# Banded attention into a maxout layer, on one core: the hand-written unit queue is replaced by another order of the same units, with other engines named for 100 of them

## The chip, the core and the metric

The kernel runs on one core of one Trainium2 chip. The time is device microseconds of that core. TensorE (PE) multiplies and transposes, with its weight loads (PEld) beside it; VectorE (DVE), ScalarE (ACT) and GpSimd (POOL) copy, cast and do arithmetic; SyncE (SP) issues nearly all DMAs. Each engine takes its instructions strictly in program order, and semaphores hold it where its input or its buffer is not ready.

## The reference

The inputs are q, k and v in float32, with 4 batches, 8 heads, 768 positions and 64 values per head. A position attends to itself and the 95 before it, and to the 8 first positions. A bias falls linearly with distance, with a slope for each head. The attention result, 3072 tokens by 512, goes through a layer that takes the largest of three products, and through one more product.

```python
scores = scale * (q @ k.T) - slope[h] * dist          # kept where global or local
a = softmax(scores)                                   # over 768 keys, most are masked
x = (a @ v).transpose(0, 2, 1, 3).reshape(3072, 512)
h = maximum(maximum(x @ w1, x @ w2), x @ w3)          # 512 -> 768
out = h @ w_out                                       # 768 -> 512
```

## The kernel before, in words

The 3072 tokens are 24 **tiles** of 128, six to a batch. Tiles 0, 6, 12 and 18 open a batch and need only their own keys; the others need the tile before as well, whose first 8 keys are overwritten with the 8 global ones. For the last layer tiles are put together in seven **chunks** of 4, 2, 2, 4, 4, 4 and 4 tiles (chunks 0 to 6 start at tiles 0, 4, 6, 8, 12, 16 and 20).

The whole program is one list of small **units** in `SCHEDULE`, read from left to right (L475 to L476). Each unit is a letter, its indices, and for many a last digit that names an engine or a way. The order of the list is the order in which each engine gets its instructions. Nothing reorders them later. The letters:

- `l`, `L`, `v`, `w`, `o` (L151 to L174, L412 to L422): loads on SP. `l` n.s is a quarter or half of the q and k of a group of tiles (0 and 1; 2 and 3; 4 and 5; 6 to 9; 10 and 11); `L` is q and k of one tile from 12 on, as two DMAs of 256 KB; `v` is the v of a tile, 256 KB; `w` and `o` are the weights. The loads `l0.0` and `l0.1` stand ahead of the list.
- `c`, `C`, `W`, `Q`: casts to bf16 by the engine of the last digit (0 ACT, 1 DVE, 2 POOL; with C of q and k, 3 is one half by DVE and one by POOL). `C`T.0 casts q and k of tile T, `C`T.1 its v.
- `x` (L226) and `X` (L245): q and k turned so that the head dimension lies on partitions. `x`, and `X` with a last digit below 4, is 8 PE transposes into PSUM and copies out of it (`X` 3 and `x` 4 split the copy between ACT and DVE). `X`T.4 is one DMA transpose issued by SP (L250).
- `S` T.g (L268): scores of tile T for 4 heads (g 0 or 1) and their exponential on ACT (L288). With a last digit 1 PE first adds the bias by two more matmuls (L275); with 0 DVE multiplies by a mask of exponentials afterwards, in `M` T.g (L302).
- `A` T (L311): 8 or 16 small matmuls P times v; DVE then takes a reciprocal and scales into `xb` (L331, L332). The last digit is the PSUM region, shared with `S` of that g, so `S` T.g waits for the DVE of an `A` there, and the reverse.
- `T` T (L335): the tile of `xb` turned into a chunk's `xT`, by 4 PE transposes and a copy (0 ACT, 1 DVE), or with 4 by a DMA transpose from SP (L340).
- `F` c.f.j (L355): 4 matmuls of chunk c for 128 columns f of weight matrix j. j = 0 is copied out by ACT (L366); j = 1 and 2 are maxima on DVE (L368, L370). A PSUM buffer, of three, is free again only then.
- `O` c.t (L385): 6 matmuls of a tile with w_out, a copy by the named engine (L382), a store by SP. `E` is the last chunk's four tiles.
- `G`, `V` put the global keys and values in place (L216, L221); `K` and `B` (L291, L297) make masks and biases from a table of distances (L451 to L470); `D` lets PE multiply zeros three times at the start.

Buffers that the steps below touch: 3 PSUM buffers `psH` for F, O and half of the transposes; one for `psT`; one each for `sp0` and `sp1`; 6 for raw q and k, 6 for raw v, 3 for `xb`.

Of the kernel before, what the change touches and what calls it, by code (L numbers as in the profile page):

```python
# [22 lines left out]


SCHEDULE = """
    K0 K1 K2 K3 K4 K5 l1.0 l1.1 D0.3 c0.0.2 B0.1 B1.1 B2.1 B3.0 K6 B4.1 B5.1 c0.1.1 c1.0.2 x0.0.4 B6.1
    B7.1 x0.1.4 S0.0.1 v0 l2.0 l2.1 K7 S0.1.1 G0.0 S1.0.1 S1.1.0 x1.0.3 c1.1.2 M0.0 M0.1 M1.0 v1 x1.1.4
    C0.1.2 v2 A0.1 G1.2 S2.0.1 M1.1 c2.0.2 x2.0.1 C1.1.1 S2.1.0 G2.2 S3.0.1 M2.0 M2.1 C2.1.1 T0.1 S3.1.1
    M3.0 M3.1 c2.1.2 v3 A1.0 C3.1.0 w0.0 V1.2 x2.1.2 w1.0 A2.1 V2.2 A3.0 T1.0 T2.1 T3.1 W1.0.1 W0.0.0
    G3.2 S4.0.0 S4.1.0 F0.0.0 F0.1.0 M4.0 F0.2.0 F0.3.0 G4.1 S5.0.0 M4.1 S5.1.0 w0.1 W0.1.1 w0.2 W0.2.2  # L30
    V3.2 F0.0.1 F0.1.1 F0.0.2 F0.1.2 v4 C4.1.0 A4.0 V4.2 w1.1 W1.1.2 W2.0.0 F0.4.0 F0.5.0 M5.0 M5.1 w1.2
    W1.2.2 v5 W2.1.0 T4.0 F0.2.1 F0.3.1 l3.0 l3.2 F0.4.1 l3.1 c3.0.2 c3.2.2 F0.5.1 o2 C5.1.0 A5.1 l3.3
    F0.2.2 Q2.2 F0.3.2 W2.2.0 o0 T5.0 F0.4.2 o1 F0.5.2 x3.0.0 F1.0.0 F1.1.0 c3.1.1 F1.2.0 x3.2.0 Q0.2
    F1.0.1 F1.1.1 F1.2.1 l4.0 l4.1 c3.3.0 F1.0.2 F1.1.2 F1.2.2 x3.1.2 x3.3.1 F1.3.0 F1.4.0 Q1.2 F1.3.1
    S6.0.0 S6.1.0 v6 v7 v8 G6.0 F1.3.2 F1.5.0 v9 c4.0.1 F1.4.1 S7.0.0 S7.1.0 G7.2 v10 M6.0 M6.1 M7.0
    M7.1 O0.0.0 F1.4.2 c4.1.1 C6.1.2 C7.1.2 L12 F1.5.1 S8.0.0 S8.1.0 x4.0.0 O0.1.0 A6.0 x4.1.2 A7.1 V7.2
    F1.5.2 v11 T6.0 O0.2.0 T7.1 G8.2 C8.1.2 S9.0.0 S9.1.0 G9.1 v12 v13 O0.3.0 F2.0.0 F2.1.0 S10.0.0 M8.0
    M8.1 M9.0 M9.1 S10.1.0 C9.1.2 L13 L14 F2.0.1 F2.1.1 F2.0.2 A8.0 C12.0.1 F2.1.2 G10.2 O1.0.0 V8.2
    A9.1 X12.1 M10.0 M10.1 C10.1.0 C11.1.0 F2.2.0 S11.0.0 S11.1.0 M11.0 M11.1 L15 F2.3.0 F2.4.0 O1.1.0
    V9.2 A10.1 F2.2.1 V10.2 T8.0 F2.3.1 F2.5.0 T9.0 A11.1 F2.4.1 T10.0 F2.2.2 F2.3.2 T11.1 F2.4.2  # L40
    S12.0.0 S12.1.0 F2.5.1 C13.0.2 C14.0.2 C15.0.1 X13.4 F3.0.0 F3.1.0 F3.0.1 G12.1 C12.1.0 F3.2.0
    F3.1.1 F3.2.1 S13.0.0 S13.1.0 F2.5.2 v14 C13.1.0 C14.1.2 M12.0 M12.1 F3.0.2 F3.1.2 X14.4 F3.2.2
    X15.4 G13.2 M13.0 M13.1 S14.0.0 S14.1.0 F3.3.0 F3.4.0 F3.5.0 M14.0 M14.1 G14.1 A12.0 A13.1 F3.3.1
    F3.4.1 F3.5.1 S15.0.0 M15.0 S15.1.0 G15.0 v15 V13.2 L16 L17 v16 T12.4 v17 M15.1 O2.0.0 C15.1.0 A14.0
    V14.2 F3.3.2 F3.4.2 T13.4 F3.5.2 C16.1.0 C16.0.2 X16.3 T14.4 C17.0.2 A15.1 X17.4 O2.1.0 S16.0.0
    S16.1.0 G16.1 L18 V15.2 L19 T15.1 M16.0 O3.0.0 M16.1 F4.0.0 F4.1.0 F4.0.1 F4.1.1 C18.0.2 L20 C19.0.2
    A16.1 F4.2.0 F4.3.0 S17.0.0 S17.1.0 F4.2.1 F4.0.2 F4.3.1 v18 M17.0 v19 M17.1 X18.3 X19.4 C20.0.0
    V16.2 F4.1.2 C17.1.2 O3.1.1 A17.1 F4.2.2 F4.3.2 S18.0.0 M18.0 S18.1.0 M18.1 F4.4.0 T16.4 T17.4
    F4.4.1 C18.1.2 C19.1.1 F4.4.2 X20.4 G18.1 S19.0.0 S19.1.0 F4.5.0 L21 M19.0 M19.1 v20 F4.5.1 A18.0
    T18.4 F4.5.2 A19.1 T19.4 V19.1 C21.0.1 X21.4 G19.1 L22 C22.0.2 L23 X22.4 O3.2.1 O3.3.0 O4.0.1  # L50
    S20.0.0 S20.1.0 M20.0 G20.0 O4.1.0 F5.0.0 F5.1.0 F5.2.0 S21.0.0 S21.1.0 G21.2 F5.0.1 F5.1.1 M20.1
    M21.0 F5.3.0 F5.0.2 F5.1.2 F5.2.1 F5.2.2 v21 C20.1.1 C21.1.2 F5.4.0 S22.0.0 M21.1 S22.1.0 C23.0.0
    F5.3.1 M22.0 M22.1 F5.5.0 F5.3.2 A20.0 V20.2 G22.2 v22 F5.4.1 X23.4 v23 F5.5.1 T20.4 A21.1 V21.1
    T21.4 F5.4.2 F5.5.2 S23.0.0 S23.1.0 M23.0 O4.2.0 M23.1 C22.1.2 A22.0 C23.1.0 O4.3.0 V22.2 T22.4
    A23.1 T23.4 O5.0.1 O5.1.0 O5.2.1 O5.3.0 F6.0.0 F6.1.0 F6.0.1 F6.0.2 F6.2.0 F6.3.0 F6.4.0 F6.1.1
    F6.2.1 F6.1.2 F6.3.1 F6.4.1 F6.2.2 F6.3.2 F6.5.0 F6.4.2 F6.5.1 F6.5.2 E
"""


# [450 lines left out]
```

## Time and profile before

| what | value |
|---|---|
| median of 3 runs | 180.5 us (180.32 to 180.64) |
| span of the profiled execution | 178.5 us |
| what lies around the span (median less span) | 2.0 us |
| instructions | 3963 |
| ACT, DVE, POOL busy | 103.2, 119.1, 37.4 us |
| loads and stores | 35.52 MB, mean 199 GB/s |
| DMA transposes: xT, qkT | 11, 9 |

The time of the profiled execution itself is not given; its span is 178.5 us, and I set it beside the median. The page cuts the span into 40 slices of 4.46 us, with a digit for the busy tenths of each engine. "Idle before" in the groups is the time in which an engine had nothing to run just before an instruction of that group, with the engine or DMA that ended it. PE's busy time is of pipelined matmuls: a matmul is listed as 379 ns long while the next one starts 216 ns later, so I count PE by starts, not by durations.

### The profile page before, as it was taken

Reading aid. Unit: us, or ns where it says so; the run is one execution under the profiler, and the core shown is the slowest. Engines: PE = TensorE matmul, PEld = TensorE weight load, DVE = VectorE, ACT = ScalarE, POOL = GpSimd, SP = SyncE. Lnnn points to the kernel's source line nnn. Section 1 sums busy time; section 2 is a strip of 40 time slices with the busy share of each in tenths; the row PEclk is TensorE's granted clock in tenths of the full one; section 3 lists DMA queues with packets and bytes.
Section 4 is the critical chain, followed back from the end, with each engine's and each line's share of the span. In section 5 each row is a group of like instructions: output and inputs, shape, how many; then the busy total and the mean of one; then the engine's idle time right before and its main releaser. Section 6 shows DMA issues by size and latency. Waiting matters only on the chain.

```text
span 178.5 us, 3963 instructions
## 1 busy us (share of the span) xinstructions
PE 167.1 (94%) x1529; PEld 95.9 (54%) x1551; DVE 119.1 (67%) x237; ACT 103.2 (58%) x160; POOL 37.4 (21%) x65
## 2 busy tenths in 40 slices
PE   3599799999999999999999999999999999999991
PEld 0455645458866677845555555454454555444451
DVE  4519975977796689748978448978358986137610
ACT  4867898646689958555753936351862543440131
POOL 4255203543343012210006024100020401000000
PEclk9999999999999999999999999999999999999998
DMA  5999999999998899899544999988989664700015
GB/s 139 292 270 243 357 321 383 319 361 356 252 194 229 218 254 227 142 204 234 92 90 122 167 253 231 145 172 152 182 156 300 123 129 147 252 12 4 0 47 190
DMA packets 83587, 35.52 MB, mean 199 GB/s; under 512 B 66160, under 2 KB 78320, under 8 KB 83568
## 3 DMA queue, kind: packets, MB, share of 16 engines
q1 hardware_dynamic: 83424, 35.20, 83.6%
q8 instruction: 12, 0.20, 0.5%
q10 hardware_dynamic: 144, 0.07, 0.1%
q14 instruction: 7, 0.06, 0.1%
HBM read 25.17 MB, written 6.29 MB: 176 GB/s over the span
## 4 chain that ended last, share of the span: by engine, by line
PE 88%; ACT 3%; DVE 2%; POOL 2%; issue 1%; DMA 1%; POOLq 0%; ACTq 0%
PE h L361 53%; PE po L376 16%; PE sp L283 7%; PE op L322 3%; PE op L325 3%; PE tpp L239 3%; PE xtp L349 2%; ACT wmask L300 2%; PE sp L275 2%; DMA out_dram<-ost 1%; DVE qkT L243 1%; DVE xb L332 1%; ACT ost L382 1%; ACT P L288 1%; PE tp L261 1%
## 5 line engine op out<-in xcount | busy, mean ns | idle before, releaser
L361 PE MATMUL h<-xT,w 128*128 128x512 bf16 (+1 forms) x491 | 99.2, 348 | 0.7 <-issue 0.2
L361 PEld LDWEIGHTS <-w 128*128 128x128 bf16 x504 | 47.0, 98 | 40.4 <-ACT w L427 0.2
L288 ACT ACTIVATE P<-sp 128x1024 bf16<-128x1024 f32 (+1 forms) x48 | 43.4, 954 | 20.4 <-PE sp L283 20.2
L368 DVE TENSOR_TENSOR h<-h,h 128x512 bf16<-128x512 bf16 (+1 forms) x42 | 25.2, 609 | 25.6 <-PE h L361 15.5
L366 ACT CAST h<-h 128x512 bf16<-128x512 f32 (+1 forms) x42 | 21.6, 532 | 21.5 <-PE h L361 21.3
L376 PE MATMUL po<-wo,ht 128*128 128x512 bf16 (+2 forms) x147 | 33.1, 362 | 0.5
L370 DVE TENSOR_TENSOR ht<-h,h 128x512 bf16<-128x512 bf16 (+1 forms) x42 | 25.0, 606 | 3.7 <-PE h L361 3.0
L307 DVE TENSOR_TENSOR P<-P,wmask 128x1024 bf16<-128x1024 bf16 x36 | 24.8, 716 | 3.6 <-ACT P L288 3.5
L382 ACT COPY ost<-po 128x512 f32<-128x512 f32 (+2 forms) x20 | 11.2, 564 | 18.4 <-PE po L376 11.2
L376 PEld LDWEIGHTS <-ht 128*128 128x128 bf16 x156 | 14.0, 98 | 13.8
L332 DVE TENSOR_TENSOR xb<-op,rz 128x512 bf16<-128x512 f32 x24 | 16.6, 691 | 0.8
L283 PEld LDWEIGHTS <-qkT 64*128 64x128 bf16 x352 | 10.2, 96 | 10.0 <-issue 8.0
L283 PE MATMUL sp<-qkT 64*128 64x128 bf16 x352 | 15.2, 223 | 0.4 <-DVE xb L332 0.4
L322 PEld LDWEIGHTS <-P 128*128 128x128 bf16 x192 | 12.5, 97 | 2.7 <-ACT P L288 0.2
L221 POOL COPY va<-vaf 8x260 int32<-8x260 int32 x14 | 6.3, 449 | 34.7 <-PE op L325 34.7
L198 POOL CAST qkb<-raw 128x1024 bf16<-128x1024 f32 x7 | 7.2, 1037 | 27.6 <-DMA raw<-in_k_dram 27.6
L322 PE MATMUL op<-va,P 128*128 128x65 bf16 x160 | 12.4, 193 | 0.3 <-ACT va L189 0.2
L239 PE MATMUL tpp<-identb,qkp 128*128 128x128 bf16 x96 | 8.5, 246 | 4.0 <-POOL qkp L183 3.5
L325 PEld LDWEIGHTS <-P 128*128 128x128 bf16 x160 | 10.4, 97 | 1.8 <-issue 0.2
L239 PEld LDWEIGHTS <-qkp 128*128 128x128 bf16 x96 | 7.0, 112 | 5.8 <-POOL qkp L183 4.4
L325 PE MATMUL op<-va,P 128*128 128x65 bf16 x128 | 9.9, 193 | 0.1
L243 ACT COPY qkT<-tpp 128x1024 bf16<-128x1024 bf16 (+1 forms) x9 | 7.9, 873 | 3.4 <-PE tpp L239 3.4
(66 smaller groups left out, 107.7 us busy)
## 6 DMA issues: line engine op xcount, KB each, us to landing
rawv<-in_v_dram SPq DMA_DIRECT2D x24, 256.0 KB, 4.9
out_dram<-ost SPq DMA_DIRECT2D x23, 256.0 KB, 2.3
rawp<-in_q_dram SPq DMA_DIRECT2D x6, 512.0 KB, 7.3
rawp<-in_k_dram SPq DMA_DIRECT2D x6, 512.0 KB, 7.7
wst<-in_moe_w_dram SPq DMA_DIRECT2D x3, 1024.0 KB, 10.3
raw<-in_q_dram SPq DMA_DIRECT2D x12, 256.0 KB, 4.2
raw<-in_k_dram SPq DMA_DIRECT2D x12, 256.0 KB, 4.7
wst<-in_moe_w_dram SPq DMA_DIRECT2D x3, 512.0 KB, 8.6
```

What stands on the lines that cost most here:

```text
L239: nc.tensor.transpose(tp[:, e, j - lo], qb["p", n, s][:, e, 2 * j:2 * j + 2].rearrange("i h d -> i (h d)"), identb)
L283: nc.tensor.matmul(sp[:, hh, j2, ds], qT(T - ds, 1)[hsl, jp], qT(T, 0)[hsl, jp], start=not how, stop=True, skip_group_check=True)
L288: nc.scalar.activation(P[:, :, 0:n], sp.rearrange("p a b d n -> p (a b) d n")[:, :, 0:n], AF.Exp, bias=0.0, scale=scale)
L307: nc.vector.tensor_mul(P, P, wmask[:, g, :, 0:2])
L322: nc.tensor.matmul(o, P[:, i, 0], heads(va[T])[:, h], start=True, stop=(t == 0), skip_group_check=True)
L325: nc.tensor.matmul(o, P[:, i, 1], heads(va[T - 1])[:, h], start=False, stop=True, skip_group_check=True)
L332: nc.vector.tensor_tensor(out=x.rearrange("p (g h) d -> p g h d", g=2), in0=o4[:, :, :, 0:64], in1=rz[:, :, :, None].to_broadcast([128, 2, ...
L361: nc.tensor.matmul(ps, w123[f // 2][:, dm, j, (f % 2) * 128:(f % 2) * 128 + 128], xT[c][:, dm], start=(dm == 0), stop=(dm == 3))
L366: nc.scalar.copy(h01, ps)
L368: nc.vector.tensor_max(h01s[c, f], h01s[c, f], ps)
L370: nc.vector.tensor_max(ht[c][:, f], h01s[c, f], ps)
L376: nc.tensor.matmul(po, ht[c][:, f, tt * 128:(tt + 1) * 128], wo[:, f, cols], start=(f == 0), stop=(f == NF - 1))
```

## The change

The functions are untouched. `SCHEDULE` holds the same 483 units in another order, and 100 of them have another last digit. Counted over both lists:

| | before | after |
|---|---|---|
| `X` by DMA, by PE | 9, 3 | 11, 1 (X16, X18 to DMA) |
| `T` by DMA, by PE | 11, 13 | 13, 11 (T9, T10 to DMA) |
| `S` with the bias by PE, by mask on DVE | 6, 42 | 8, 40 |
| `V` on ACT, DVE, POOL | 0, 2, 14 | 7, 3, 6 |
| `C` on ACT, DVE, POOL, split | 12, 7, 17, 0 | 7, 9, 18, 2 |
| `O` copied by ACT, DVE | 15, 5 | 12, 8 |
| `B` on ACT, DVE, POOL | 1, 7, 0 | 3, 2, 3 |

With the bias by PE before: S0.0, S0.1, S1.0, S2.0, S3.0, S3.1. After: S0.1, S1.0, S1.1, S2.0, S2.1, S3.0, S3.1, S4.0. The loads at the start go from l0, l1, v0, l2, v1, v2, v3, w0.0 to l0, l1, v0, v3, v1, v2, l2, w0.0. All eight K and three B stand ahead of the first copy on ACT, where it was seven K and one B. In PE's order x1.0 comes ahead of S1, and A0 ahead of x1.1. The list's first lines, and the places that the prediction speaks of:

```diff
-    K0 K1 K2 K3 K4 K5 l1.0 l1.1 D0.3 c0.0.2 B0.1 B1.1 B2.1 B3.0 K6 B4.1 B5.1 c0.1.1 c1.0.2 x0.0.4 B6.1
-    B7.1 x0.1.4 S0.0.1 v0 l2.0 l2.1 K7 S0.1.1 G0.0 S1.0.1 S1.1.0 x1.0.3 c1.1.2 M0.0 M0.1 M1.0 v1 x1.1.4
-    C0.1.2 v2 A0.1 G1.2 S2.0.1 M1.1 c2.0.2 x2.0.1 C1.1.1 S2.1.0 G2.2 S3.0.1 M2.0 M2.1 C2.1.1 T0.1 S3.1.1
-    M3.0 M3.1 c2.1.2 v3 A1.0 C3.1.0 w0.0 V1.2 x2.1.2 w1.0 A2.1 V2.2 A3.0 T1.0 T2.1 T3.1 W1.0.1 W0.0.0
-    G3.2 S4.0.0 S4.1.0 F0.0.0 F0.1.0 M4.0 F0.2.0 F0.3.0 G4.1 S5.0.0 M4.1 S5.1.0 w0.1 W0.1.1 w0.2 W0.2.2
...
-    V14.2 F3.3.2 F3.4.2 T13.4 F3.5.2 C16.1.0 C16.0.2 X16.3 T14.4 C17.0.2 A15.1 X17.4 O2.1.0 S16.0.0
...
-    T18.4 F4.5.2 A19.1 T19.4 V19.1 C21.0.1 X21.4 G19.1 L22 C22.0.2 L23 X22.4 O3.2.1 O3.3.0 O4.0.1
-    S20.0.0 S20.1.0 M20.0 G20.0 O4.1.0 F5.0.0 F5.1.0 F5.2.0 S21.0.0 S21.1.0 G21.2 F5.0.1 F5.1.1 M20.1
...
+    K3 K6 K4 K1 K2 K5 B1.0 B4.0 K7 B0.2 K0 B7.1 B2.2 B5.0 B6.2 B3.1 l1.0 l1.1 c0.0.1 D0.3 c1.1.2 c0.1.1 v0
+    x0.0.3 x0.1.2 S0.1.1 v3 M0.1 S0.0.0 c1.0.1 x1.0.1 G0.2 S1.1.1 C0.1.1 S1.0.1 M1.1 M0.0 M1.0 A0.1 v1
+    G1.2 x1.1.4 S2.0.1 C1.1.1 S2.1.1 G2.2 S3.0.1 S3.1.1 v2 C2.1.2 A1.0 l2.0 V1.0 T0.0 l2.1 M3.1 w0.0
+    C3.1.2 M2.0 G3.1 M2.1 A2.1 T1.1 c2.0.2 V2.0 x2.0.2 c2.1.2 w1.0 M3.0 A3.0 x2.1.4 W0.0.2 T2.0 w0.1 T3.1
+    S4.0.1 M4.0 S4.1.0 W1.0.1 F0.0.0 F0.1.0 F0.3.0 F0.2.0 w0.2 v4 M4.1 G4.1 S5.1.0 W2.0.0 S5.0.0 W0.2.1
...
+    F2.5.2 A9.0 F2.2.1 F2.1.1 F2.2.2 S11.1.0 M11.1 V9.1 S11.0.0 M11.0 T8.0 T9.4 O1.1.0 F2.4.0 A10.1 T10.4
+    C13.1.0 X12.0 F2.1.2 F2.4.1 C15.0.2 V10.2 A11.1 F2.3.0 F2.3.1 F2.4.2 F2.3.2 T11.1 F2.0.1 C13.0.2
+    F2.0.2 v12 S12.1.0 M12.1 S12.0.0 G12.0 M12.0 C15.1.1 X13.4 F3.0.0 F3.0.1 F3.2.0 F3.2.1 F3.2.2 X15.4
+    S13.1.0 M13.1 S13.0.0 C12.1.2 v19 F3.3.0 F3.3.1 F3.5.0 A12.0 v14 M13.0 C14.0.2 X14.4 F3.5.1 F3.3.2 L16
+    C16.0.1 G13.0 S14.0.0 M14.0 S14.1.0 G14.2 F3.0.2 F3.1.0 M14.1 v20 C14.1.1 A13.0 V13.2 F3.1.1 F3.1.2
+    L19 F3.5.2 T12.4 v21 L17 C17.0.2 S15.0.0 M15.0 v17 S15.1.0 L18 v16 v18 G15.2 F3.4.0 F3.4.1 X16.4
+    C18.0.2 F3.4.2 A14.0 M15.1 C17.1.0 T13.4 T14.4 O2.0.0 O2.1.0 V14.1 A15.0 O3.0.0 L20 C20.0.2 X17.4
+    T15.1 S16.1.0 S16.0.0 G16.1 O3.1.1 M16.1 X18.4 F4.0.0 C16.1.1 F4.5.0 F4.0.1 M16.0 V15.1 F4.5.1 F4.1.0
...
+    A19.1 V19.2 T19.4 C21.0.3 F4.3.2 C22.0.0 C21.1.2 O3.2.1 S20.1.0 X22.4 S20.0.0 G20.1 O4.0.1 M20.0 X21.4
+    F5.0.0 F5.2.0 L23 F5.1.0 M20.1 A20.0 F5.4.0 C23.1.0 V20.0 F5.4.1 T20.4 F5.1.1 S21.1.0 S21.0.0 G21.1
...
+    F5.3.2 O4.3.0 O5.1.0 M23.1 M23.0 A23.0 T23.4 O5.2.1 O5.3.0 O5.0.0 F6.0.0 F6.3.0 F6.3.1 F6.3.2 F6.0.1
```

In program counts PE has 20 instruction pairs fewer: 24 transposes go (8 each of X16 and X18, 4 each of T9 and T10) and 4 bias matmuls come (2 for each of two more S). In the profile of the changed kernel a function's line is one lower than here, since the list is one line shorter.

More of the change, by code (lines that the diff above doesn't have):

```diff
@@ L31 @@
[L31 to L44, printed above, removed]
-    V14.2 F3.3.2 F3.4.2 T13.4 F3.5.2 C16.1.0 C16.0.2 X16.3 T14.4 C17.0.2 A15.1 X17.4 O2.1.0 S16.0.0
@@ L46 @@
[L46 to L49, printed above, removed]
-    T18.4 F4.5.2 A19.1 T19.4 V19.1 C21.0.1 X21.4 G19.1 L22 C22.0.2 L23 X22.4 O3.2.1 O3.3.0 O4.0.1
@@ L51 @@
-    S20.0.0 S20.1.0 M20.0 G20.0 O4.1.0 F5.0.0 F5.1.0 F5.2.0 S21.0.0 S21.1.0 G21.2 F5.0.1 F5.1.1 M20.1
[L52 to L55, printed above, removed]
@@ L56 @@
-    F6.2.1 F6.1.2 F6.3.1 F6.4.1 F6.2.2 F6.3.2 F6.5.0 F6.4.2 F6.5.1 F6.5.2 E
+    K3 K6 K4 K1 K2 K5 B1.0 B4.0 K7 B0.2 K0 B7.1 B2.2 B5.0 B6.2 B3.1 l1.0 l1.1 c0.0.1 D0.3 c1.1.2 c0.1.1 v0
[3 more added lines that the diff above has]
+    S4.0.1 M4.0 S4.1.0 W1.0.1 F0.0.0 F0.1.0 F0.3.0 F0.2.0 w0.2 v4 M4.1 G4.1 S5.1.0 W2.0.0 S5.0.0 W0.2.1
@@ new lines @@
+    W0.1.2 V3.0 w1.1 w1.2 F0.0.1 F0.0.2 C4.1.2 F0.1.1 F0.1.2 A4.0 W2.1.0 M5.0 v5 W1.1.2 V4.2 F0.4.0 F0.5.0
+    M5.1 F0.3.1 W1.2.0 F0.4.1 F0.5.1 W2.2.0 T4.1 C5.1.0 F0.3.2 l3.0 F0.5.2 l3.3 A5.0 c3.0.0 c3.3.2 F0.2.1
+    F0.4.2 T5.0 F0.2.2 l3.1 c3.1.2 x3.3.2 x3.0.1 l3.2 F1.0.0 F1.2.0 F1.5.0 F1.1.0 v7 c3.2.2 x3.2.0 C7.1.1
+    F1.1.1 F1.1.2 o2 Q2.2 F1.4.0 x3.1.4 o1 F1.2.1 o0 F1.2.2 Q0.2 S6.0.0 S6.1.0 G6.0 F1.0.1 F1.0.2 l4.0
+    S7.0.0 Q1.1 M6.0 v6 l4.1 S7.1.0 G7.2 v8 F1.3.0 F1.4.1 O0.0.0 M7.0 S8.1.0 c4.0.2 L12 S8.0.0 G8.1 F1.4.2
@@ new lines @@
+    M7.1 C6.1.2 x4.0.0 M6.1 L14 c4.1.2 O0.1.0 A6.1 F1.5.1 v10 A7.0 V7.2 F1.3.1 v13 F1.3.2 v11 C8.1.0 T6.0
+    v9 C9.1.2 x4.1.3 S9.0.0 M9.0 L15 S9.1.0 G9.0 M8.1 v15 T7.0 O0.2.1 F1.5.2 M8.0 L13 O0.3.1 S10.0.0 M10.0
+    S10.1.0 M9.1 M10.1 C12.0.3 F2.0.0 O1.0.0 F2.1.0 A8.0 C10.1.2 C11.1.1 F2.2.0 V8.0 G10.2 F2.5.0 F2.5.1
+    F2.5.2 A9.0 F2.2.1 F2.1.1 F2.2.2 S11.1.0 M11.1 V9.1 S11.0.0 M11.0 T8.0 T9.4 O1.1.0 F2.4.0 A10.1 T10.4
+    C13.1.0 X12.0 F2.1.2 F2.4.1 C15.0.2 V10.2 A11.1 F2.3.0 F2.3.1 F2.4.2 F2.3.2 T11.1 F2.0.1 C13.0.2
@@ new lines @@
+    T15.1 S16.1.0 S16.0.0 G16.1 O3.1.1 M16.1 X18.4 F4.0.0 C16.1.1 F4.5.0 F4.0.1 M16.0 V15.1 F4.5.1 F4.1.0
+    X20.4 F4.0.2 C19.0.1 X19.4 A16.1 V16.0 F4.2.0 C19.1.2 F4.2.1 S17.0.0 S17.1.0 F4.3.0 M17.1 F4.3.1
+    F4.1.1 M17.0 S18.0.0 M18.0 C18.1.2 L22 v23 S18.1.0 M18.1 F4.1.2 T16.4 G18.1 S19.0.0 M19.0 S19.1.0
+    O3.3.1 G19.0 F4.2.2 L21 A18.0 T18.4 F4.4.0 M19.1 F4.4.1 A17.1 C20.1.0 F4.4.2 v22 F4.5.2 T17.4 C22.1.2
+    A19.1 V19.2 T19.4 C21.0.3 F4.3.2 C22.0.0 C21.1.2 O3.2.1 S20.1.0 X22.4 S20.0.0 G20.1 O4.0.1 M20.0 X21.4
@@ new lines @@
+    F5.0.0 F5.2.0 L23 F5.1.0 M20.1 A20.0 F5.4.0 C23.1.0 V20.0 F5.4.1 T20.4 F5.1.1 S21.1.0 S21.0.0 G21.1
+    M21.1 C23.0.2 F5.1.2 F5.4.2 F5.0.1 F5.5.0 S22.1.0 S22.0.0 G22.2 M21.0 F5.5.1 M22.1 F5.5.2 M22.0 F5.0.2
+    A21.0 F5.3.0 F5.2.1 X23.4 V21.0 T21.4 F5.2.2 F5.3.1 O4.1.0 A22.0 V22.2 T22.4 O4.2.1 S23.0.0 S23.1.0
+    F5.3.2 O4.3.0 O5.1.0 M23.1 M23.0 A23.0 T23.4 O5.2.1 O5.3.0 O5.0.0 F6.0.0 F6.3.0 F6.3.1 F6.3.2 F6.0.1
+    F6.0.2 F6.1.0 F6.1.1 F6.1.2 F6.2.0 F6.4.0 F6.4.1 F6.2.1 F6.2.2 F6.4.2 F6.5.0 F6.5.1 F6.5.2 E
```

## The prediction

> **What bounds the kernel now.** I read the page's busy shares first, then the waits of PE in the stretch from 23.3 us to the end, then a table by stage, and last the timelines of the start.
>
> ```profile
> PE 167.1 (94%) x1529; PEld 95.9 (54%) x1551; DVE 119.1 (67%) x237; ACT 103.2 (58%) x160; POOL 37.4 (21%) x65
> ...
> PE   3599799999999999999999999999999999999991
> ```
>
> PE has 9 in every slice from the sixth to the last but one, so the start and PE's own work are all there is to gain. The waits of PE alone between 23.3 and 175 us (us in total, times, longest) and a table of three stretches (busy us and instructions of each engine, clock, DMA share, GB/s) say it sharper:
>
> ```profile
> PE h L361 <- issue: 0.2, 1, 0.2
> ```
>
> ```profile
> 13.30:19.60 6.30, 5.84 (x91) 3.65 (x89) 6.23 (x12) 4.99 (x6) 2.63 (x4) 1.00 1.25 264
> 19.60:23.30 3.70, 2.82 (x61) 2.32 (x61) 3.04 (x7) 3.18 (x5) 0.55 (x2) 1.00 1.06 376
> 23.30:172.00 148.70, 147.49 (x1301) 83.60 (x1321) 104.18 (x195) 83.74 (x128) 28.14 (x42) 1.00 0.82 190
> ```
>
> From the first F at 23.3 us PE never waits again but for 0.2 us. So the time is: when F0 starts, plus PE's work from there, plus any wait that the new order brings, plus a tail (E) that does not change. The span is 178.5 us, the median 180.5; I carry the 2.0 us between them over.
>
> **PE's work from F0 on.** The price of a transpose is in the chain of waits, in order of time (start, us, what):
>
> ```profile
> 7.69 1.01 PE tpp L239 x8
> ...
> 16.37 0.54 PE sp L275 x2
> ...
> 65.91 0.45 PE tp L261 x8
> ...
> 70.54 0.22 PE xtp L349 x4
> ```
>
> X16 and X18 go to DMA: 2 x 0.45 = 0.90 us. T9 and T10: 2 x 0.22 = 0.44. All four lie behind F0, where nothing hides a PE instruction, so **1.34 us goes**. F, O, S, A and E keep their counts. Blocks of S between other work number 19 in both lists behind F0, so the change of pace at their edges costs the same. On the other side of the sum, S1.1, S2.1 and S4.0 get a bias by PE (0.54 us for two matmuls), S0.0 loses its own: all ahead of F0, counted next. The units moved between ACT, DVE and POOL cost PE nothing as long as PSUM buffers come free in time (below).
>
> **The start.** It is a race of DMA landings and ACT. Casts that had waited for a DMA tell when it landed: q and k of tiles 0 and 1 at 5.09 and 6.87 us, of tiles 2 and 3 at 8.70 and 10.56, v0 at 11.71. So 512 KB takes about 1.8 us and a v 1.15. ACT, which sets the pace until all eight score tiles are through (start, us):
>
> ```profile
> 8.31 0.59 ACT L243 COPY qkT<-tpp 128x512 bf16<-128x512 bf16 x1 [0.67 <-PE tpp L239]
> 9.50 0.60 ACT L288 ACTIVATE P<-sp 128x512 bf16<-128x512 f32 x1 [0.60 <-PE sp L283]
> ...
> 11.87 1.94 ACT L288 ACTIVATE P<-sp 128x1024 bf16<-128x1024 f32 x2 [0.77 <-PE sp L283]
> 13.70 0.59 ACT L243 COPY qkT<-tpp 128x512 bf16<-128x512 bf16 x1
> 15.10 1.02 ACT L288 ACTIVATE P<-sp 128x1024 bf16<-128x1024 f32 x1 [0.81 <-PE sp L283]
> 16.41 3.12 ACT L288 ACTIVATE P<-sp 128x1024 bf16<-128x1024 f32 x3 [0.29 <-PE sp L283]
> ```
>
> The last exponential (S3.1) ends at 19.5. I walk the new order with these durations.
> - Eight K and three B on ACT from 3.76 us, at 0.43 each (2.59 for six): free at 8.45. This is hidden, since PE ends x0.1 at 8.6 in both lists. POOL's three B aren't in the trace; between a DVE one (0.35) and a POOL cast of 128x512 (0.7) three cost 1.1 to 2.1 us from 3.7, done before PE wants them at 8.6. Nothing at either end.
> - x0.1's copy is now one of 1.01 on ACT, not two halves beside each other: done at 9.66 where the halves were done by 9.4. S0.1 then S0.0, first exponential at 10.15 (was 9.50).
> - x1.0 now precedes S1 on PE (0.9 us at the slow early pace), then the bias and matmuls of S1.1: its exponential at 12.7, S1.0's until 14.65. Before, both had ended by 13.8. **0.85 late.**
> - A0 waits for the region of S1.1 (13.7), x1.1 follows A0, ACT's half of its copy runs 14.7 to 15.25. S2.0 is ready at 15.75, and then ACT runs S2.0, S2.1, S3.0, S3.1 back to back, at 0.97: done at 19.65. The gaps of 0.81 and 0.29 above are gone, and with them the delay: 0.1 late.
> - Now v. v1, v2 and v3 stand ahead of l2, so all four v are there by 15.1, where the last was there only at 19.77 (an ACT cast waited 0.23 for it). But A1, A2, A3 also need S3.1's end and the PSUM of S3, so this gains little: A1 at 18.8, A2 at 19.75. For it l2 lands 3.4 us later (at about 16.9 and 18.8 to 19.6, for 13.5 and at most 16.5); its POOL casts (1.04 each) end by 18.0 and 20.6, still ahead of x2.0 and x2.1 on PE.
> - Behind it: T1 and x2.0 stand ahead of A3, V2 sits on ACT (about 0.35: between POOL's 0.39 and a 0.2 copy of G) behind T0's copy, so A3 starts at 21.05 (was 20.44), its xb ends at 22.65, T3's copy waits for DVE's half of x2.1 and ends at 23.7; S4.0 with its new 0.43 to 0.54 us of bias and S4.1 end at 24.05.
>
> F0 starts at 24.1 instead of 23.27: **0.8 us later.** Bounds: 0.2 if the bias of S4.0 still fits into PE's idle time ahead of T3 (PE has 0.9 us idle from 19.6 to 23.3), 1.5 if the slow pace of PE lasts longer. w0.0 lands at the same place in the queue, as the bytes ahead of it are the same.
>
> One sentence apart: the rows show eight transposes in 1.01 us at 7.69 and in 0.45 at 65.91, though the page's clock row says full speed in both slices. [...]
>
> **What could make PE wait behind F0.** I set each unit at its place in PE's work and looked at who must be ready.
> - PSUM buffers: a matmul group is 0.86 us (0.44 in chunks 1 and 2), an eviction 0.69 on DVE and 0.59 on ACT (0.42 and 0.39), with three buffers. The fullest stretch of DVE is 53 to 58 us, 7.0 us of work in 5 (O0.2 and O0.3 are copied by DVE now); ahead of it DVE has room, and I find A9 held by A8's scaling by about 0.3 us. The next are 83 to 88 (5.9) and 113 to 118 (6.4). Before, the fullest was 5.9, and it held nothing. I take 0.2 us for all.
> - DVE's cast C16.0 stands in the queue behind L16, and a late L16 would stop all evictions behind it. L16 lands about 83, DVE gets there about 85.
> - DMA around 72 to 98 us: from v12 to X16's transpose SP issues 16 loads of 256 KB, four X and one T. At the 243 GB/s of the window from 100 to 110 us (DMA share 1.12, full) 256 KB takes 1.08 us; 20 x 1.08 + 0.5 from 72.0, with 2.4 to 3.3 from issue to landing (T and X in the page's list of issues): X16 lands between 96 and 98, S16 wants it at 97.5; T14 a microsecond behind it, F4 wants it at 99.4. **This is the narrowest place**, and 0 to 1.5 us there is open.
> - T19 (A19 at 118, scaled at about 120.5, DMA 2.4) lands at 122.9, F5 wants it at 123.0; before, F5 stood 6 us behind A19, now 4.5. 0 to 0.8. T23 has about 0.4 to spare.
>
> **Sum.** 178.5 + 0.8 - 1.34 + 0.1 = 178.0 us; with 2.0 around it **180.0**.
>
> **Rivals.**
> 1. *Late transposes (slower).* X16, T14 or T19 lands late, and S16, F4 or F5 holds PE, behind which everything queues. From 0.5 us of such waits the gain is used up. For it: the queue is 84% busy in the page, four transposes and 16 loads stand before S16, and SP takes them in order. Against: three full-looking stretches before (share over 1.0) held PE nowhere. Price 0.6 to 2.5 us: 180.6 to 182.5. 29%.
> 2. *The start isn't late.* S4's bias and x1.0 hide in PE's idle time: 178.5 + 0.1 - 1.34 = 177.3, or 179.3. For it: ACT, which set the pace, ends S3.1 at the same time. Against: A3 stands behind two more PE units. 23%.
> 3. *The v move does nothing.* This is inside both: only 0.23 us of waiting for v shows before, so what it promises can't be more than that.
>
> My own case has 43%: 179.7 to 180.4. Something else, DVE's bursts above all, 5%, above it. The range takes in rival 2 and most of rival 1: 178.9 to 182.0. Faster by over 0.2% means below 180.14, which is also about what a measurement of this kernel can tell from no change: 23 from rival 2, 30 of my 43: 53%. Within 0.2%: 13 and 4 of the late ones: 17%. Slower: 30%.
>
> **What will show it.** The first F at about 24.1 us; S3.1's exponential ends at 19.6 or so; 24 PE transposes fewer (L260 with 8, L348 with 44); PE's waits behind F0 below 0.5 us in all. I am wrong if PE waits for a DMA transpose at S16, F4 or F5, if the first F comes before 23.5 or after 24.8, or if DVE's queue holds F.

## The result, and the profile after

The changed kernel takes 186.77 us (median of 4 runs, 186.33 to 187.5), the kernel before beside it 180.49. The ratio is 1.036 (95% interval 1.033 to 1.038): **slower by 6.3 us**, on the other side of zero from the forecast of 180.0 and above its range. The profiled execution took 186.67 us, with a span of 184.9. In the times below, executions that took over 1.5% more than the fastest of their kernel are left out (one of e3, two of e7, two of e10, of these e10's profiled one).

The same views as in the prediction, first the busy shares and the slices of the page of the changed kernel (a slice is now 4.62 us; lines of functions are one lower than before):

```profile
PE 169.1 (91%) x1531; PEld 95.1 (51%) x1531; DVE 119.6 (65%) x235; ACT 101.1 (55%) x159; POOL 39.7 (21%) x62
...
PE   3589999999999999989999399999999999999991
...
DMA  5999999999919999999999999899993126510015
```

Before, the row of DMA was this:

```profile
DMA  5999999999998899899544999988989664700015
```

PE now has a 3 in the 23rd slice (102 to 106 us). DMA has a 1 in the 12th (51 to 55), and then 9 nearly all the way to the 30th, where before it had 5, 4 and 4 in the 20th to 22nd. PE's waits from the first F at 25.3 us on, as this view answers for 25 to 182 us (total, times, longest, us):

```profile
PE sp L282 <- DMA qkT<-qkb: 3.2, 3, 2.8
PE h L360 <- DMA xT<-xb: 1.3, 1, 1.3
PE op L321 <- POOL va L188: 0.5, 1, 0.5
```

Before, the same view had one line, 0.2 us. Now PE waits at A9 (67.9 us, for the cast of v9), at F3 (79.4, for T10), at S16 (105.7, for X16), and a little at S17 and S19 (for X17 and X19). I add the waits up as start of one matmul to start of the next, less what the same step takes where nothing waits: 0.62 + 1.33 + 2.89 + 0.24 + 0.26 = 5.34 us. The first weight load of F0 comes at 25.29 us for 23.23. So 2.06 + 5.34 - 1.34 (the transposes) = 6.06; the first weight load of E is 6.23 us later. If the 1.34 us did go, which e16 and e18 below bear out, the start and the waits are the result to within 0.2 us.

**The start**, as ACT shows it (start, us):

```profile
10.42 1.09 ACT L287 ACTIVATE P<-sp 128x512 bf16<-128x512 f32 x2 [0.49 <-PE sp L282]
12.99 1.02 ACT L287 ACTIVATE P<-sp 128x1024 bf16<-128x1024 f32 x1 [1.49 <-PE sp L282]
14.50 1.02 ACT L287 ACTIVATE P<-sp 128x1024 bf16<-128x1024 f32 x1 [0.48 <-PE sp L282]
...
16.77 3.98 ACT L287 ACTIVATE P<-sp 128x1024 bf16<-128x1024 f32 x4 [0.71 <-PE sp L282]
```

I had walked S1.1 to 12.7 and the four back to back from 15.75; they come at 12.99 and 16.77. Every wait here is for PE. The chain of waits shows PE's pace (start, us, what):

```profile
7.84 1.05 PE tpp L238 x8
...
10.59 0.97 PE tpp L238 x8
```

Eight transposes still took 0.85 us at 15.01, for 0.46 at 21.95. PE went at its slow pace until about 15.7 us, where before it sped up at 13.3. How much of the 2.06 us that explains is answered further down, from e14.

**SP's queue.** What SP issues, and when (start, us; the 1.93 is how long SP was at it):

```profile
46.03 1.93 SPq L173 DMA_DIRECT2D rawv<-in_v_dram  x1
53.59 0.36 SPq L382 DMA_DIRECT2D out_dram<-ost  x1
54.05 1.39 SPq L166 DMA_DIRECT2D raw<-in_q_dram  x1
```

From 47.96 to 53.59 SP stands behind the store of O0.0, whose data aren't ready, with L12, L14, v10 and the rest behind it. That is the 1 in DMA's row. From L12's first half (58.24) to X16 (105.65) 41 transfers land, one every 1.2 us on average.

### The profile page after: what moved, and what is told of

Its sections match the earlier page's. It is cut to its first block, busy times and chain, and to the rows that moved or that the text cites. A ratio compares the mean times of both kernels' runs of the same rounds, so it can differ in the third digit from the quotient of the medians.

```text
span 184.9 us, 3933 instructions
## 1 busy us (share of the span) xinstructions
PE 169.1 (91%) x1531; PEld 95.1 (51%) x1531; DVE 119.6 (65%) x235; ACT 101.1 (55%) x159; POOL 39.7 (21%) x62
## 4 chain that ended last, share of the span: by engine, by line
PE 70%; DMA 12%; SPq 5%; ACT 4%; DVE 4%; issue 3%; POOL 1%; DVEq 0%; ACTq 0%; POOLq 0%
PE h L360 41%; PE po L375 13%; PE sp L282 6%; DMA raw<-in_k_dram 3%; PE tpp L238 3%; DMA rawp<-in_k_dram 3%; DMA xT<-xb 3%; PE op L321 2%; ACT P L287 2%; PE op L324 2%; PE sp L274 2%; SPq L249 2%; DMA qkT<-qkb 2%; ACT qkT L242 1%; SPq L339 1%
## 5 line engine op out<-in xcount | busy, mean ns | idle before, releaser
L360 PE MATMUL h<-xT,w 128*128 128x512 bf16 (+1 forms) x504 | 100.7, 349 | 1.3 <-DMA xT<-xb 1.3
L367 DVE TENSOR_TENSOR h<-h,h 128x512 bf16<-128x512 bf16 (+1 forms) x42 | 25.4, 609 | 20.9 <-PE h L360 15.9
L375 PE MATMUL po<-wo,ht 128*128 128x512 bf16 (+2 forms) x156 | 33.9, 363 | 0.0
L369 DVE TENSOR_TENSOR ht<-h,h 128x512 bf16<-128x512 bf16 (+1 forms) x42 | 25.5, 610 | 4.7 <-PE h L360 3.0
L306 DVE TENSOR_TENSOR P<-P,wmask 128x1024 bf16<-128x1024 bf16 x33 | 22.8, 707 | 6.2 <-ACT P L287 6.0
L381 ACT COPY ost<-po 128x512 f32<-128x512 f32 (+2 forms) x17 | 9.4, 560 | 14.3 <-PE po L375 12.8
L321 PE MATMUL op<-va,P 128*128 128x65 bf16 x160 | 12.6, 193 | 0.7 <-POOL va L188 0.5
L330 DVE RECIPROCAL rz<-op 128x8 f32<-128x8 f32 x24 | 4.9, 203 | 10.6 <-PE op L324 8.2
L381 DVE COPY ost<-po 128x512 f32<-128x512 f32 (+1 forms) x9 | 5.8, 645 | 8.0 <-PE po L375 8.0
L188 POOL CAST va<-rawv 128x512 bf16<-128x512 f32 x8 | 5.0, 634 | 25.4 <-DMA rawv<-in_v_dram 15.6
```

The source lines that it names most:

```text
L306: nc.vector.tensor_mul(P, P, wmask[:, g, :, 0:2])
L321: nc.tensor.matmul(o, P[:, i, 0], heads(va[T])[:, h], start=True, stop=(t == 0), skip_group_check=True)
L360: nc.tensor.matmul(ps, w123[f // 2][:, dm, j, (f % 2) * 128:(f % 2) * 128 + 128], xT[c][:, dm], start=(dm == 0), stop=(dm == 3))
L367: nc.vector.tensor_max(h01s[c, f], h01s[c, f], ps)
L369: nc.vector.tensor_max(ht[c][:, f], h01s[c, f], ps)
L375: nc.tensor.matmul(po, ht[c][:, f, tt * 128:(tt + 1) * 128], wo[:, f, cols], start=(f == 0), stop=(f == NF - 1))
```

## The experiments

Three theories were open first. **H**: the standstill behind O0.0's store is the cause. **V**: DMA is given more work than it has time for, in whatever order. **S**: the start counts by itself. A fourth, **Q**, came of the first runs: the order of SP's queue. "After" is the changed kernel, "before" the one before. Each run has before's beside it (180.38 to 180.46 in every set). The waits at single places are again from start to start, as above.

### e1_loads_first

```diff
-  O0.0.0 M7.0 S8.1.0 c4.0.2 L12 ... M6.1 L14 ... F1.5.1 v10 ... T6.0 v9
+  L12 L14 v10 v9 O0.0.0 M7.0 S8.1.0 c4.0.2 ... M6.1 ... F1.5.1 ... T6.0
```

> The kernel after, with the loads L12, L14, v10 and v9 moved ahead of O0.0 in the list, so that SP issues them before it waits for O0.0's store. Theory H (SP sat from 48 to 53.6 us behind that store, DMA ran dry for about 4 us, and all waits of PE behind F0 come of it): no dry stretch around 48 to 56 us, the waits at A9, F3 and S16 (5.8 us with S17 and S19) shrink to under 1.5 us, time 186.8 - 4.5 = about 182. Theory V (the list simply asks for more by DMA before S16 than fits, wherever the dry stretch is): S16 still waits 2 us or more, time above 185. Theory S (only the start matters) says nothing of this run: F0 stays at 25.3.

Measured: 186.02 us. The dry stretch is gone, and with it the waits at A9, F3, S17 and S19, 2.5 us in all. S16 still waits, 3.2 us, so by the letter of the expectation this is V. H explains four waits of five but not the longest, and the time fell by 0.75 only: from F0 to E the profile gains 0.53 us. A part of the rest lies in the clock (columns: us, busy by engine, granted clock of PE, DMA share, GB/s):

```profile
100.00:104.00 4.00, 0.94 (x8) 0.40 (x6) 0.81 (x2) 0.59 (x1) 1.04 (x1) 1.00 1.39 189
104.00:108.00 4.00, 3.69 (x24) 1.72 (x26) 0.95 (x3) 1.94 (x2) 0.00 (x0) 0.61 0.80 227
```

Right behind the wait for X16 PE is granted 0.61 of its clock, taken over 4 us; in the profiled execution of the changed kernel it was 1.00 there.

### e2_transposes_pe

```diff
-  T9.4 ... T10.4 ... X16.4 ... X18.4
+  T9.0 ... T10.1 ... X16.3 ... X18.3     (nearer to where PE needs them)
```

> The kernel after, with T9, T10, X16 and X18 transposed by TensorE again, at their places in the order of before. Theory V (the added DMA transposes are what makes DMA late): the waits at F3 and S16 go, PE gains 1.34 us of transposes; 186.8 - 4.8 + 1.34 = about 183. Theory H (the lost 4 us of DMA are the cause, the transposes only the first that show it): F4 waits for T13 and T14 instead of S16 for X16, and F3 for T11's side or X13; the waits lose 1 to 2 us and 1.34 us of work comes back: 185.5 to 187.

Measured: 189.53 us (187.8 to 190.2). S16 no longer waits, nor F4. But the places where I put the transposes brought waits of their own: 2.1 us at T9 (for ACT's copy), 0.8 within T11, 1.4 at S18 (for DVE's copy of X18). Inconclusive on V: it only shows that S16 doesn't wait where X16 is turned by PE.

### e3_start_before and e4_both

```diff
-  K3 K6 K4 ... (after's list up to the first F)
+  K0 K1 K2 ... (before's list up to the first F)       e4: also the edit of e1
```

> The kernel after, with the first part of the list (up to the first F) in the order of before; the loads l2, v1 to v3 are thus in the old order as well. Theory S (the start costs its own 2.06 us): F0 at 23.2 to 23.3, and the time falls by 2.06 if PE sets the pace behind it: 184.7. If the waits behind F0 are fixed in time by DMA (SP's store of O0.0 comes 2 us earlier too, but the queue from 53.6 on is full), S16's wait grows by up to 2 us: 185 to 186.8.

> The start of before (as in the run before this one) and the four loads ahead of O0.0. H and S together: PE's waits behind F0 under 1.5 us, F0 at 23.3, 186.8 - 2.06 - 4.5 = about 180.2, near the kernel before, and 179.2 (faster by the 1.34 us of transposes) if no wait is left. Theory V: S16 waits 2 us or more and it stays above 183.

Measured: 185.65 and 184.4 us. F0 stands at 23.4 in both, 1.9 earlier; S16 waits 2.7 and 3.4. The two edits together gain 2.4 of the 6.3. The wait at S16 belongs to neither.

### e5_queue_order

```diff
-  v19 ... v20 ... L19 ... v21 ... v18 ... X16.4 ... T13.4 T14.4 ... X17.4
+  X16.4 ... T13.4 T14.4 v18 L19 v19 ... X17.4 v20 v21          (on e4)
```

> The kernel of the run before with both edits (start of before, four loads ahead of O0.0), and now v18, L19 and v19 moved behind T14, v20 and v21 behind X17: five units, seven transfers fewer ahead of X16. Theory V, made precise: what stands in SP's queue between T10 (which F3 needs) and X16 (which S16 needs) takes 27 us to land, and PE has only 23 us of work between F3 and S16, so S16 waits for the queue, whatever is done ahead of it. Seven loads of 1.2 us fewer: X16 lands 8 us before S16 wants it, T13 and T14 in time, all waits behind F0 under 1 us in all, no fall of the clock: 184.4 - 4.3 - 1.8 = about 178.5, ahead of the kernel before. If the added transposes themselves are too much (the rival), T14 or X17 to X19 hold PE by 2 us or more and it stays above 181.

Measured: 183.82 us. X16 lands at 97.4 and S16 doesn't wait. Now S17, S18 and S19 do, for X17, X18 and X19, 1.7 + 0.8 + 1.1 us, and 0.6 behind them: by the letter of the expectation the rival. But L20, v20, v21 and X20 stood ahead of X19, where before's list has v20 and v21 behind it.

What had landed by 106 us spoke against V. Counting 256 KB or one transpose as one, the weights `w` left out, after had 81 transfers in, and before 77: after was **ahead**. It had 22 v and before 18, while X16, T13 and T14 were just coming. That led to Q.

### e6_before_dma4

```diff
-  T8.0 F2.3.1 F2.5.0 T9.0 A11.1 F2.4.1 T10.0 ... T12.4 ... C16.0.2 X16.3 ... X18.3
+  T8.0 T9.4 F2.3.1 F2.5.0 T10.4 A11.1 F2.4.1 ... C16.0.2 X16.4 T12.4 ... X18.4   (on before)
```

> The kernel before, with T9, T10, X16 and X18 by DMA, X16 and its cast moved ahead of T12, and nothing else. If the four transposes are worth what the prediction gave them and before's queue has room for them: 180.45 - 1.34 = 179.1, PE's waits as before. If a DMA transpose costs the queue more than it frees PE from: X18 or T10 hold PE by 1 us or more, 180 or above.

Measured: 180.37 us, ratio 1.000 (0.999 to 1.001). The four added transposes harm nothing in before's order: no S and no later F waits. They gain nothing either, as F3 now waits 0.8 us at its second matmul and the start of this profile came 0.4 later.

### e7_v_first_alone

```diff
-  v0 l2.0 l2.1 K7 ... v1 ... v2 ... v3
+  v0 v1 v2 v3 l2.0 l2.1 K7 ...           (on before)
```

> The kernel before with v1, v2 and v3 moved ahead of the second group's q and k in SP's queue, and nothing else: the part of the change that its description names first. It frees at most the 0.23 us that an ACT cast waited for v3, and l2 lands 3.4 us later, which x2.0 and x2.1 on PE wait for unless their slack takes it: between -0.2 and +1.5 us, 180.2 to 181.9. If most of the 2.06 us at the start of the changed kernel came of this part, it is 181.5 or more; if of the order on ACT and PE, 180.9 or less.

Measured: 186.2 us (ratio 1.032, 1.030 to 1.034), far outside. The part that the description names first costs about 5.8 us when it is put into before's list. x2.0 stands ahead of A1 on PE there, and PE waits for its cast with all else queued behind it:

```profile
PE tpp L239 <- POOL qkp L183: 3.2, 1, 3.2
```

Then the clock falls to half from 19 to 22.5 us (0.76, 0.50 and 0.88 granted in the three windows of 2 us from 18 us on), F0 starts at 27.4, and one F behind it (F0.5.1) waits another 1.9 us for DVE. After's list has x2.0 behind A1 and T0, where no wait for l2 shows: the move needs the rest of the new start.

### e8_fill_wait, e9_warm_start, e11_warm_after, e12_warm_before

```diff
e8  (on e1)     -  T15.1 S16.1.0          +  T15.1 D0.14 S16.1.0
e9  (on after)  -  D0.3                   +  D0.10
e11 (on after)  -  D0.3, x0.0.3, x0.1.2   +  D0.10, x0.0.3 D0.6, x0.1.2 D0.3
e12 (on before) -  D0.3, x0.0.4           +  D0.11, x0.0.4 D0.4
```

> The kernel after with the four loads ahead of O0.0, and 14 matmuls of zeros (3.0 us of work that the result doesn't use) put in front of S16, where PE otherwise waits 3.3 us. Clock theory: the fall of the granted clock to half for some 3 us right behind that wait (104 to 108 us in the run without the filling) comes of the wait; with PE busy there it doesn't come, and the time falls by 1.0 to 1.8 to 184.2 to 185, though PE does more. If the clock falls for another reason, the time stays at 186.0, or rises by what of the 3.0 us sticks out.

> The kernel after with ten matmuls of zeros at the start in place of three, so that PE is busy from 1.2 to 5.5 us, where it idled for 3 us. Clock theory of the start: the transposes and bias matmuls at half pace until 15.7 us come of PE's idle start; with PE busy the pace doubles from the first or second group of transposes on (0.45 for eight in place of 1.0), S3.1's exponential ends about 1 us earlier and F0 starts at 24 to 24.5 in place of 25.3; the time falls by up to 1, less what the waits at F3 and S16 take back. If the late start comes of ACT's order alone, F0 stays at 25.3.

> The kernel after with ten matmuls of zeros in place of three at the start, six behind the first group of transposes and three behind the second, to keep PE's clock up where ten alone let it fall again from 8.5 to 15.4 us. If PE's slow early pace is what made the start 1.3 us later than the walk, F0 starts at 24 to 24.4 in place of 25.3. The waits for X16 behind it stay, so the time says little: 185 to 187.

> The kernel before with eleven matmuls of zeros in place of three at the start and four more behind the first group of transposes. If PE's slow pace until 13.3 us sets the start of this kernel too, F0 comes 0.3 to 1 us earlier: 179.4 to 180.1. If the landings and ACT set it, 180.4; if the clock falls again after 8 us, as it did in the changed kernel with ten, 180.4 or later.

Measured: 186.85, 187.44, 187.53 and 180.47 us. In e8 the clock stays up; the same windows as for e1 above:

```profile
100.00:104.00 4.00, 3.88 (x21) 1.79 (x20) 0.95 (x2) 0.58 (x1) 1.04 (x1) 1.00 1.81 168
104.00:108.00 4.00, 2.11 (x24) 1.19 (x25) 0.23 (x2) 1.67 (x2) 0.00 (x0) 1.00 0.73 203
```

The mean clock was 1.00 in all four executions, where e1 had 0.988 to 0.991. So at S16 the clock fell where PE idled for 3.2 us (e1), and not where the zeros left 2.0 us of idling (e8). The time didn't fall: in this profile X16 landed 1.8 us later than in e1, though SP issued it only 0.3 us later; why stays open.

e9 shows the slow pace of the start in the clock row. Its timeline lists eight transposes with 0.62 us at 5.71 and 7.85 us, and with 1.03 at 10.12:

```profile
8.00:12.00 4.00, 3.13 (x30) 1.80 (x30) 2.34 (x3) 2.48 (x4) 1.34 (x3) 0.59 1.29 250
12.00:16.00 4.00, 4.00 (x39) 2.23 (x40) 2.40 (x6) 2.58 (x3) 0.21 (x1) 0.55 1.28 241
```

In e11 PE is kept busy there, and the same windows read full speed; eight transposes are listed with 0.61 us at 8.05 and 0.62 at 10.09:

```profile
8.00:12.00 4.00, 3.80 (x42) 2.04 (x40) 2.42 (x4) 2.78 (x5) 1.59 (x3) 1.00 1.29 250
12.00:16.00 4.00, 3.45 (x47) 1.90 (x46) 2.48 (x6) 3.46 (x5) 0.71 (x3) 1.00 1.27 243
```

F0 starts at 23.35, **1.94 us earlier** than in after, with the order of the units kept: at full speed from about 7 us on, the new start isn't late. Of the gain 0.8 us is left in the profiled execution (185.87 us), as the waits behind F0 are about 1 us longer (S16's is 3.6); the other three took 187.0 to 188.3, at mean clocks of 0.977 to 0.991. In before's list the same filling changes nothing (ratio 1.002, 1.000 to 1.004): F0 stays at 23.23, as x2 waits for its cast and A1 for v1.

So the clock fell behind waits of 3.2 us in e1 and e7, and it stayed up at S16 in e8 and at the start of e11, where PE was kept busy (1.00 in the windows above). The last section has a fall behind shorter waits, and waits of 2.9 and 3.6 us without one.

### e10_due_order, e13_due_to_the_end, e15_due_but_stalled, e16_t19_first

```diff
e10 (on e5)   +  T14.4 X17.4 O2.0.0 O2.1.0 L19 ... X18.4 O3.0.0 v18 ... v19 ... X19.4 L20 C20.0.2 v20 ... X20.4 v21
e13 (on e10)  +  C18.1.2 C20.0.2 ... T16.4 G18.1 X20.4 ... L21 ... v20 L22 ... T18.4 ... v21 ... T17.4 v22 ... T19.4 v23
e15 (on e13)  +  L12, L14, v10 and v9 behind O0.0 again, as in after
e16 (on e13)  +  T16.4 G18.1 L21 X20.4 ... v20 ... T18.4 ... T17.4 ... T19.4 C21.0.3 X21.4 L22 v21 ... X22.4 ... L23 v23 v22
```

> The kernel with the start of before and the four loads ahead of O0.0, and now SP's queue between T10 and X20 in the order in which PE wants the results: X17, L19, X18, v18, v19, X19 ahead of L20, v20, X20 and v21. Theory Q (not the amount that DMA carries but its order is wrong: at 106 us the changed kernel has landed 81 transfers and the kernel before 77, yet X16 and X17 to X19 are late since v17 to v21 and L19, which PE wants 10 to 40 us later, stand ahead of them): PE's waits behind F0 fall from 4.3 to under 1 us, and with the 1.34 us of transposes it comes to 179.3, ahead of the kernel before. Theory V (DMA has more work than time up to S19, whatever the order): the wait moves once more, to S20 or F5, and it stays above 182.

> The run before with the order by need carried on to the last tiles: the cast C20 behind C18 on GpSimd, X20 behind T16, L21, v20, L22, v21, v22 and v23 each behind what is wanted sooner. Theory Q (order): no wait of PE above 0.5 us behind F0 but the 0.3 at F3; F0 at 23.0 to 23.4; 179 to 179.6, ahead of the kernel before by the transposes. Theory V (amount): a wait of 2 us or more in front of S20, F5 or S22, 182 or above.

> The order by need to the end, as in e13, but L12, L14, v10 and v9 behind O0.0 again, as in the changed kernel: SP stands still for about 4 us there. Theory H in what is left of it: the waits at A9 (0.6) and F3 (1.0 to 1.5) come back and nothing else: 1.5 to 2.2 us above e13. If the standstill costs nothing once the order is right, the same time as e13.

> The run with the order by need (e13), and now L22, v21, v22, v23, L23 behind T19, X21 directly behind it, L21 ahead of X20, and the casts that belong to them (C22, C23 on GpSimd) behind that. Theory Q: PE's wait in front of F5 was four to five transfers of 1.2 us that stood ahead of T19, so it falls from 5.9 to under 1 us; with F0 at 23.4, PE's own work less 1.34 us, the clock up: 179.3 to 180.0, at or ahead of the kernel before. Theory V (amount): 2 us or more of waits in front of S21, S22 or F6, above 182.

Measured: 187.4 (186.11 and 188.68), 188.05, 189.94 and 180.4 us. Two misses came first, and by the letter of their expectations both are V. In e10 no S from S16 to S19 waits any more. But I had put the cast of L20 on GpSimd ahead of that of v18, so A18 waited 1.4 us. S20 waited 2.2 us for A19's result, which DVE held for 3.1 us until a late DMA transpose (`xT<-xb`) freed an `xb`, and F5 2.2 for T19; the clock fell among them, to 0.68 over 122 to 138 us. In e13 PE's wait behind F0 is, but for 0.3 us at F3, gathered at one place, F5, which waits for T19:

```profile
PE h L361 <- DMA xT<-xb: 5.9, 1, 5.9
```

L22, v21 and v22, four transfers of 1.2 us that PE wants more than 10 us later, and four more had been queued ahead of T19. e15 answers H: 1.9 us more than e13, as forecast, with waits at A9 (0.9), F3 (0.9, where e13 has 0.3) and a piece of 0.4 within A10. In e16 the three units go behind T19 (and the casts of C22.0 and C23.1 from ACT to GpSimd), and the 5.9 us are gone; what is left is 0.5 at F3 and 0.4 in front of A19 at 120 us. F0 to E is 0.49 us shorter than before, and with these 0.85 us of waits that is the 1.34 of the transposes. The ratio to before is 1.000 (0.998 to 1.001): with before's start and a queue in order of need, the changed order costs nothing. V is out: the bytes, the transposes and, from F0 on, PE's order are those of after.

### e14_start_alone, e18_after_but_queue, e17_before_x16_x18

```diff
e14  after's list up to the first F, then before's
e18  after's list up to the first F, then e16's
e17 (on before)  -  T12.4 ... C16.0.2 X16.3 ... X18.3   +  C16.0.2 X16.4 T12.4 ... X18.4
```

> The first part of the list, up to the first F, as in the changed kernel; all behind it as in the kernel before. It prices the start alone. F0 at 25.3, no new wait behind it, so 180.4 + 2.06 = 182.5 (182.1 to 182.9). If the late start is partly taken back behind F0, by loads that have landed meanwhile, 181 to 182; there is little to take back, as PE waits 0.2 us in all there.

> The changed kernel with its own start, and from the first F on the list of the run with T19 first (e16): the changed order of TensorE's work, the changed transposes, but SP's queue by need. If start and queue are all there is: 180.4 + 1.8 = 182.2 (181.8 to 182.7). If the two hang together (the later start shifts what SP has to wait for), 183 or more, or 181 or less.

> The kernel before with X16 and X18 alone by DMA (X16 and its cast ahead of T12), T9 and T10 on TensorE as before. If the gain was lost only at T9 and T10 (F3 waited 0.8 us there in the run with all four): 180.45 - 0.9 = 179.5. If X16 and X18 give nothing either, 180.2 to 180.5: then PE's freed time is taken back elsewhere, by S18's wait for X18 or at the end.

Measured: 182.28 us (ratio 1.011, 1.009 to 1.013); 181.51 (1.006, 1.005 to 1.008); 180.05 (0.998, 0.997 to 0.999). The start alone costs 1.8 us, with F0 at 24.77 in e14 and 24.91 in e18; after, e1, e2 and e8 have the same start, and F0 at 24.9 to 25.4. In e18 PE waits for nothing between F0 and 180 us that the view lists, and from F0 to E takes 144.88 us, 1.14 less than before: here the transposes come through. It keeps the start and PE's order of the change and all its engines but those of two casts, so 186.77 - 181.51 = **5.3 us is SP's queue**, with the casts that go with the loads moved in it. Over before it is 1.0 us: in its profiled execution, the lowest of the four, 1.68 at F0 less 1.14 behind it, and 0.2 behind E. e17, the last term by itself, is the fastest kernel of the study: 0.90 us of transposes fewer, F0 to E 0.88 shorter, and 0.4 us of it in the time, since F0 came 0.24 later in its profile and the rest lies behind E.

## Why the prediction was wrong

- **The transposes, right.** 1.34 us were priced; 1.14 were had from F0 to E (e18), and in e16 0.49 with 0.85 of waits.
- **The start, wrong in size.** 0.8 us was forecast, bounds 0.2 and 1.5; the profile has 2.06, e14 prices it at 1.8. The failed term is "ACT, which sets the pace": in after's rows of ACT every wait is for PE. I walked ACT from before's durations and let PE reach its fast pace at 13.3 us, as before. But e14, which has the new start, was as early at the fast pace (PE's timelines of 5 to 26 us; the first two rows are e14's, the others after's), and its F0 still comes 1.5 us late:

```profile
14.36 0.61 PE L239 MATMUL tpp<-identb,qkp 128*128 128x128 bf16 x8
24.77 1.47 PE L361 MATMUL h<-xT,w 128*128 128x512 bf16 x6
...
14.82 1.04 PE L238 MATMUL tpp<-identb,qkp 128*128 128x128 bf16 x8
25.30 1.04 PE L360 MATMUL h<-xT,w 128*128 128x512 bf16 x4
```

In e14 x0.1's transposes end at 8.9 us where I had 8.6, ACT's four in a row begin at 16.04 (walked: 15.75), A3 starts at 21.45 (21.05), and DVE ends A3's xb at 23.40 (22.65). That is the 0.7 us by which the walk was short. After's profile adds 0.5 us, as its slow pace lasts to 15.7. The bound of 1.5, for a slow pace that lasts longer, was an estimate.
- **v ahead of l2.** "Does nothing" held only beside the units that moved with it: x2.0 behind A1. Alone it costs 5.8 us (e7).
- **The narrowest place was the right place, the sum there was not.** "20 x 1.08 + 0.5 from 72.0" put X16 at 96 to 98; it landed at 105.65. v12, the first of these transfers, was issued at 75.9, not 72.0, and landed 4.5 us later, at 80.41; the next twenty, up to X16, took 25.2 us, 1.26 each. The 1.08 came from a window (100 to 110 us) in which five loads, two stores and one DMA transpose land; this stretch has five transposes in it, and whether they are the reason no run shows. e4 has neither the late start nor the standstill, and there too the twenty take 25.4 us and S16 waits 3.4. S16 wanted X16 at 102.8 instead of 97.5, so PE waited 2.9. In the sum this wait and all others behind F0 stood at 0.1 us, though the list above it left up to 1.5 open here; they took 5.3.
- **The step that I left out.** I set each transfer beside the unit that waits for it, but not SP beside the stores that it stands behind. SP's 5.6 us behind O0.0 were in the list to be read. They cost 0.75 us in after's own queue (e1) and 1.9 in e13's (e15), not all, as I first thought.
- **The rivals.** Rival 1 (late transposes, 29%, to 182.5) was the mechanism: S16, S17 and S19 waited 3.4 us for theirs. F3's wait for T10 and A9's for v9, 2.0 us, it didn't name. Its price was too low, as I took the waits for single ones: when S16's was taken away it came up at S17 to S19 (e5), and then at S20 and F5 (e10, e13).
- **PSUM, C16 behind L16, T19, T23.** Nothing to see there, where 0.2 us and up to 0.8 had been allowed: A9's wait was for v9's cast and not for DVE, and F5 didn't wait.

Of the prediction's signs of being wrong two showed: F0 came after 24.8, and PE waited for a DMA transpose at S16.

Open: why X16 took 1.8 us longer in e8, and how much of the time of single executions is the fallen clock. In after's profiled execution the clock fell only in the last 2 us (0.55 over 183.0 to 184.9), in its other three the mean was 0.987 to 0.991, and the times hardly differ.

## What to carry to other kernels

Where one engine issues all transfers in order, list them by the time at which their result is wanted, and price every transfer that is wanted late but stands early as a delay of all behind it (here 1.2 us each): a DMA that is busy all the time can be ahead in bytes and late where it counts (here 81 transfers for 77 by 106 us, with PE waiting 2.9 us for X16). Check at the same time what the issuing engine itself has to wait for (here 5.6 us behind one store). And a move that looks free on one engine may idle PE, after which PE can run at half speed for as long again (in e7 3.2 us of waiting, then half speed from 19 to 22.5 us).

## What the runs showed of the hardware that I had not expected

- A wait of PE of some 3 us can cost more than itself: behind 3.2 us (e1) the clock was granted at 0.5 for 3.4 us (0.72, 0.50 and 0.93 in the windows of 2 us from 104 us on), some 1.7 us of PE's work; in and behind the 5.9 us of e13 for 6.8 us (0.96, 0.50, 0.50, 0.50 and 0.83 from 126 us on). With PE kept busy by matmuls of zeros it didn't fall (e8, 1.00). But it needn't fall: after's profiled execution waits 2.9 us at S16, e11's 3.6, and both keep 1.00. Nor does it take one long wait: in e5 it fell behind the three at S17 to S19, none above 1.7 us, with PE busy for half of the stretch ahead (columns as for e1):

```profile
113.25:116.66 3.41, 1.71 (x23) 0.78 (x24) 3.21 (x7) 1.09 (x2) 0.00 (x0) 1.00 0.96 192
116.66:120.07 3.41, 3.19 (x20) 1.38 (x16) 0.78 (x2) 2.04 (x3) 0.00 (x0) 0.50 1.17 234
```

- The page's clock row reads 1.00 at the start of before and after while PE goes at half pace (eight transposes in 1.01 and 1.05 us, later in 0.45 and 0.46); in e9, where eight had taken 0.62 us and then took 1.03 (as listed in its timeline), it reads 0.59 and 0.55. The length of a transpose is the safer reading.
- SP can be held in issuing: X16's transpose took 3.23 us to issue, T13's 1.22 (chain of waits of after). In after the transposes X took 1.2 to 1.5 us to issue where the last transfer under way landed up to 3.3 us later, and 3.2 and 3.9 where it was 4.7 and 5.2 (X16, X17); whether what is under way is what holds SP, no run tests:

```profile
100.16 3.23 SPq L249
...
103.49 1.22 SPq L339
```
